# A hand-written order of 24 token blocks on five engines: a new order table, 11 transposed copies and 9 last sums moved to VectorE

## The chip, the cores and the metric

The kernel runs on one core of a Trainium2 chip. The metric is the device time of the core in microseconds (us), and the runs before have a median of 119.65 us (118.96 to 119.69, three runs). The profile used throughout is one execution of the same program, whose span is 118.6 us.

## What is computed

Windowed attention with four sink keys, followed by a highway layer. Cut to what matters:

```python
scores = q @ k.T / sqrt(64)          # 4 batches, 8 heads, 768 positions, head size 64
keep = (key < 4) | (0 <= row - key < 128)
a = softmax(where(keep, scores, -1e9))
x = (a @ v) as [3072 tokens, 512]
H = maximum(x @ w_h, 0)
T = 1 / (1 + exp(-(x @ w_t + b_t)))
out = T * H + (1 - T) * x            # float32
```

## The kernel before

The 3072 tokens are 24 blocks of 128, six to a batch. Each block goes through a fixed set of steps, and a table of text, `_STEPS`, lists every step of every block as `name:block`. The program is recorded in the order of that table, so each engine executes its own steps in exactly that order, and an instruction that waits holds up everything behind it on its engine. Buffers come from rotating pools.

The steps, with the lines of the profile and the engine:

- `lq`, `lk` load 128 rows of q and k for all heads (L151, GpSimd's queue, 128 KB each with a cast to f16; blocks 0 and 1 come through the SP and ACT queues, L144, and are cast on VectorE by `cvq`, `cvk`, L169). `lv` loads v of one block of batch 0 (L147), `lv0` and `lv1` half of v of a later batch (L157, 384 KB each). `lw_t`, `lw_h` load the weights (L181).
- `T` transposes q and k on TensorE (L267), `cT` copies the result to SBUF on ScalarE (L273).
- `S0`, `S1` are the scores of four heads each (TensorE, L317), `E0`, `E1` the exponentials (ScalarE, L325), `M0`, `M1` the multiplication by the mask (VectorE, L336, in place in `e`).
- `sk`, `es` and `pks` handle the sink keys; `pks` has two small copies (L284) and, from the second batch on, a product (L176) on GpSimd. `BA` opens the accumulations with the bias of the gate (L342) and the sink part (L350).
- `AV` is the product with v (TensorE, L370); `rec` and `x` divide by the sum (VectorE, L379, L384).
- `X` transposes x on TensorE (L395), `cX` copies the result from PSUM to SBUF on ScalarE (L406).
- `Tt` and `H` are the two products of the highway layer (TensorE, L416 and L428); `u` is a tanh on ScalarE (L421); `d`, `g`, `ee` are VectorE's part (L434, L441, L447).
- `o` is the last sum (L453), on GpSimd for all blocks but the last, which is on VectorE; the store to memory is issued on the SP queue behind it (L454).

`_FILL` adds idle matmuls on a constant tile in front of a few early steps. The pools that matter: 8 buffers each for the loaded q and k, 2 PSUM buffers that `T` and `S` share, one PSUM buffer that `AV` and `X` share, 2 PSUM buffers for `Tt`, `H`, the bias and `sk`, and 4 buffers for the last sum. GpSimd's loads use eight semaphores in turn, so a load is issued when the one eight places ahead of it has landed.

Of the kernel before, what the change touches and what calls it, by code (L numbers as in the profile page):

```python
# [11 lines left out]
ALU = mybir.AluOpType  # L12
# [6 lines left out]

_FILL = {'T:0': 4, 'S1:0': 3, 'T:1': 1, 'S1:1': 3, 'S0:1': 2, 'S1:2': 1, 'T:3': 3}  # L20
_STEPS = """
    lq:0 lk:0 lq:1 lk:1 K3:0 lsv:0 pm:0 K1:0 lbt:0 cvq:0 K4:0 cvk:0 lv:1 K2:0 lv:0 pb:0 T:0
    cvq:1 cT:0 S1:0 BA:1 cvk:1 S0:0 lq:2 E1:0 E0:0 M0:0 M1:0 T:1 lk:2 cT:1 lw_t:0 S1:1 T:2 lq:3
    lk:3 E1:1 M1:1 AV:0 pks:0 lw_h:0 lq:4 rec:0 x:0 cT:2 S0:1 E0:1 S1:2 M0:1 E1:2 X:0 lk:4 cX:0
    K5:0 lv:2 T:3 S0:2 AV:1 cT:3 Tt:0 E0:2 lv:3 S1:3 rec:1 u:0 x:1 X:1 E1:3 sk:2 M0:2 es:2 M1:2
    cX:1 H:0 T:4 d:0 S0:3 cT:4 M1:3 BA:2 lq:5 lk:5 AV:2 Tt:1 lv:4 lq:6 S1:4 E0:3 rec:2 x:2 X:2
    g:0 M0:3 lv:5 H:1 ee:0 u:1 lk:6 g:1 cX:2 lq:7 T:5 E1:4 BA:3 AV:3 d:1 S0:4 cT:5 rec:3 E0:4
    Tt:2 u:2 x:3 sk:4 es:4 S1:5 X:3 ee:1 M1:4 T:6 M0:4 cX:3 E1:5 g:2 lv0:6 H:2 lk:7 o:0 d:2
    BA:4 AV:4 S0:5 Tt:3 cT:6 rec:4 S1:6 x:4 ee:2 E0:5 lk:8 lq:8 X:4 u:3 H:3 T:7 M0:5 lq:9 M1:5
    cX:4 E1:6 BA:5 S0:6 cT:7 AV:5 d:3 Tt:4 E0:6 rec:5 x:5 S1:7 u:4 X:5 g:3 H:4 T:8 cX:5 E1:7  # L30
    ee:3 o:1 lv1:6 cT:8 BA:6 lk:9 M1:6 lq:10 o:2 M0:6 d:4 AV:6 lk:10 rec:6 S0:7 lq:11 x:6 M1:7
    Tt:5 E0:7 g:4 o:3 S1:8 M0:7 X:6 u:5 H:5 cX:6 BA:7 ee:4 T:9 AV:7 pks:6 d:5 E1:8 cT:9 rec:7
    S0:8 x:7 g:5 E0:8 Tt:6 lk:11 sk:8 S1:9 M1:8 X:7 T:10 u:6 M0:8 H:6 es:8 cX:7 o:4 BA:8 ee:5
    lq:13 d:6 E1:9 AV:8 rec:8 x:8 S0:9 cT:10 Tt:7 X:8 lq:12 lk:12 g:6 S1:10 H:7 E0:9 u:7 cX:8
    E1:10 T:11 M0:9 o:5 M1:9 BA:9 AV:9 lk:13 S0:10 ee:6 lv0:12 Tt:8 cT:11 d:7 sk:10 rec:9 E0:10
    x:9 o:6 u:8 X:9 S1:11 g:7 T:12 lk:14 M0:10 lq:15 ee:7 es:10 cX:9 H:8 E1:11 M1:10 BA:10 d:8
    lq:14 AV:10 rec:10 x:10 g:8 cT:12 S0:11 Tt:9 M1:11 E0:11 X:10 u:9 S1:12 o:7 M0:11 lv1:12
    cX:10 lk:15 H:9 BA:11 ee:8 T:13 E1:12 S0:12 cT:13 AV:11 d:9 rec:11 Tt:10 x:11 E0:12 lq:16
    u:10 S1:13 M0:12 X:11 H:10 g:9 T:14 cX:11 M1:12 o:8 BA:12 E1:13 ee:9 cT:14 lq:17 d:10 AV:12
    S0:13 Tt:11 rec:12 x:12 lk:16 o:9 M1:13 X:12 E0:13 M0:13 g:10 S1:14 u:11 T:15 H:11 cX:12  # L40
    AV:13 BA:13 ee:10 E1:14 d:11 pks:12 rec:13 S0:14 Tt:12 cT:15 x:13 lk:17 M1:14 sk:14 X:13
    S1:15 E0:14 g:11 u:12 es:14 T:16 H:12 cX:13 M0:14 ee:11 BA:14 E1:15 o:10 AV:14 d:12 rec:14
    S0:15 cT:16 x:14 g:12 lk:18 E0:15 Tt:13 X:14 u:13 M1:15 S1:16 lq:18 H:13 M0:15 T:17 lq:19
    cX:14 E1:16 g:13 cT:17 BA:15 ee:12 AV:15 S0:16 d:13 o:11 Tt:14 E0:16 rec:15 lv0:18 lk:19
    sk:16 x:15 u:14 ee:13 X:15 S1:17 cX:15 o:12 T:18 es:16 M0:16 lk:20 E1:17 M1:16 lq:20 lq:21
    g:14 H:14 BA:16 AV:16 S0:17 Tt:15 cT:18 d:14 S1:18 rec:16 x:16 E0:17 u:15 ee:14 M0:17 o:13
    X:16 H:15 T:19 cX:16 E1:18 lv1:18 BA:17 M1:17 cT:19 S0:18 AV:17 Tt:16 S1:19 d:15 rec:17
    E0:18 lk:21 o:14 x:17 g:15 X:17 u:16 M0:18 T:20 cX:17 M1:18 H:16 ee:15 E1:19 AV:18 BA:18
    d:16 rec:18 x:18 S0:19 Tt:17 cT:20 S1:20 E0:19 X:18 H:17 M1:19 u:17 T:21 M0:19 g:16 lq:22
    cX:18 ee:16 AV:19 BA:19 lk:22 E1:20 g:17 S0:20 o:15 cT:21 pks:18 rec:19 Tt:18 E0:20 d:17  # L50
    sk:20 x:19 u:18 M1:20 es:20 ee:17 S1:21 lq:23 X:19 cX:19 T:22 M0:20 E1:21 H:18 d:18 o:16
    BA:20 AV:20 rec:20 x:20 cT:22 S0:21 E0:21 Tt:19 X:20 M1:21 S1:22 g:18 u:19 H:19 cX:20 lk:23
    T:23 M0:21 BA:21 E1:22 g:19 ee:18 AV:21 o:17 S0:22 cT:23 E0:22 d:19 rec:21 Tt:20 sk:22 x:21
    u:20 es:22 X:21 S1:23 M1:22 cX:21 M0:22 ee:19 H:20 BA:22 E1:23 AV:22 g:20 d:20 S0:23 rec:22
    Tt:21 E0:23 x:22 M1:23 u:21 M0:23 X:22 H:21 cX:22 ee:20 BA:23 d:21 o:18 AV:23 rec:23 x:23
    g:21 ee:21 Tt:22 u:22 X:23 g:22 H:22 o:19 cX:23 Tt:23 d:22 H:23 ee:22 d:23 u:23 g:23 o:20
    o:21 ee:23 o:22 o:23
"""


# [1 line left out]
def kernel(  # L62
# [27 lines left out]
    NB = NT // P  # L90
# [164 lines left out]
    xtp_of, xh_of, xT_of, t_of, u_of, h_of, dd_of, ee_of, sk_of = {}, {}, {}, {}, {}, {}, {}, {}, {}  # L255
# [49 lines left out]
    def scores(n, g):  # L305
        qT, kT = qkT[n]
        srcs = ([] if n % NSC == 0 else [qkT[n - 1][1]]) + [kT]
        np_ = len(srcs)
        sps = s_ps.tile([P, 2, 512], FP32, tag="s", name="sps")
        fill(sps[:, 0, :], f"S{g}:{n}")  # L310
        for hl in range(2):
            hp = 2 * g + hl
            for pc, kk in enumerate(srcs):
                for hh in range(2):
                    rows = slice(64 * hh, 64 * hh + 64)
                    o = (hl * np_ + pc) * P
# [120 lines left out]

    def g(n):
        gt = td_pool.tile([P, DM], FP16, tag="gt", name="gt")
        eng = nc.gpsimd if False else nc.vector  # L440
        eng.tensor_scalar(out=gt, in0=u_of.pop(n), scalar1=0.5, scalar2=0.5,  # L441
                          op0=ALU.mult, op1=ALU.add)
        g_of[n] = gt

    def ee(n):
# [1 line left out]
        nc.vector.tensor_tensor(out=e, in0=g_of.pop(n), in1=dd_of.pop(n), op=ALU.mult)  # L447
# [63 lines left out]
```

## Time and profile before

| | |
|---|---|
| median of the runs | 119.65 us |
| span of the profiled execution | 118.6 us |
| TensorE matmul busy | 105.6 us (89%) |
| VectorE busy | 94.6 us (80%) |
| ScalarE busy | 93.3 us (79%) |
| GpSimd busy | 90.2 us (76%) |

The span is the time from the first to the last instruction of the program in the trace; the device time is about 1.0 us more (119.65 against 118.6). A row of a group says how long one instruction takes (mean), how often it occurs, and how long its engine was idle just ahead of it. From the groups, mean of one: `e` multiplied by the mask, 128x1024, 828 ns; the division `xh` 691 ns; `dd` 685 ns; `gt` 371 ns; `ee` 419 ns; the last sum on GpSimd 1188 ns, and on VectorE (block 23 alone) 691 ns; the copy `xT` on ScalarE 582 ns. The idle time ahead of an instruction counts only on the engine that sets the end.

### The profile page before, as it was taken

The page shows a single profiled execution, that of the slowest core. Times are in us where ns is not written, and L with a number is a line of the kernel's source. Part 1 is how long each engine was busy: PE and PEld are TensorE (multiplying, and loading weights), DVE is VectorE, ACT ScalarE, POOL GpSimd, SP SyncE. Part 2 cuts the span into 40 slices and gives each one's busy share as a digit, 9 for nine tenths or more (in the row PEclk, how much of TensorE's full clock was granted, in tenths as well). Part 3 has the DMA queues.
Part 4 walks back from the last instruction along what each step waited for, and adds up shares of the span by engine and source line. Part 5 has one row for each costly group of instructions (what it writes and reads, how often), then busy time and mean ns, then how long its engine had stood idle before and what let it go on. Part 6 is the DMA issues. An engine that isn't in the chain of part 4 may idle for free.

```text
span 118.6 us, 3872 instructions
## 1 busy us (share of the span) xinstructions
PE 105.6 (89%) x1617; PEld 57.7 (49%) x1617; DVE 94.6 (80%) x204; ACT 93.3 (79%) x129; POOL 90.2 (76%) x105
## 2 busy tenths in 40 slices
PE   5947899999996899999998999999699999999920
PEld 2313465556462456555554664555454664644300
DVE  5497458789899739688987997999989969878760
ACT  2137899899978479999989999999869999963410
POOL 5999995999999884969998799699949651233430
PEclk9999999999999679999999999999999999999999
DMA  2999999999999999899999999999999692220242
GB/s 49 248 171 182 173 194 154 161 150 151 196 211 172 224 122 135 131 100 194 159 165 205 162 136 116 177 197 161 151 212 152 44 144 85 94 88 0 88 177 88
DMA packets 79540, 17.56 MB, mean 148 GB/s; under 512 B 75426, under 2 KB 76450, under 8 KB 79524
## 3 DMA queue, kind: packets, MB, share of 16 engines
q0 software_dynamic: 71904, 9.98, 127.2%
q1 hardware_dynamic: 5540, 6.82, 16.6%
q10 hardware_dynamic: 2080, 0.52, 2.4%
q8 instruction: 12, 0.20, 0.7%
q14 instruction: 4, 0.03, 0.1%
HBM read 21.01 MB, written 6.29 MB: 230 GB/s over the span
## 4 chain that ended last, share of the span: by engine, by line
PE 37%; POOL 25%; DMA 20%; issue 7%; DVE 6%; ACT 1%; POOLq 0%; DVEq 0%
DMA vb<-in_v_dram 14%; PE hps L428 10%; PE tps L416 9%; POOL qsd L151 7%; DMA wh_sb<-in_moe_w_h_dram 6%; POOL ksd L151 6%; PE av L370 6%; PE sps L317 5%; POOL otok L453 5%; DVE e L336 3%; POOL vb L157 2%; POOL v_all L147 2%; PE xtp L395 2%; PE tp L267 2%; PE tps L342 2%
## 5 line engine op out<-in xcount | busy, mean ns | idle before, releaser
L325 ACT ACTIVATE e<-sps 128x1024 f16<-128x1024 f32 (+1 forms) x48 | 46.0, 964 | 4.6 <-PE sps L317 4.2
L453 POOL TENSOR_TENSOR otok<-xh,ee 128x512 f32<-128x512 f16 x23 | 27.3, 1188 | 20.1 <-DVE ee L447 16.9
L336 DVE TENSOR_TENSOR e<-e,mask 128x1024 f16<-128x1024 f16 (+1 forms) x48 | 36.4, 784 | 3.4 <-ACT e L325 3.1
L273 ACT COPY qk<-tp 128x1024 f16<-128x1024 f16 x24 | 24.5, 1022 | 6.3 <-PE tp L267 6.1
L416 PE MATMUL tps<-wt_sb,xT 128*128 128x512 f16 x96 | 25.5, 389 | 0.0
L428 PE MATMUL hps<-wh_sb,xT 128*128 128x512 f16 x96 | 25.4, 388 | 0.0
L434 DVE SCALAR_TENSOR_TENSOR dd<-hps,xh 128x512 f16<-128x512 f32 x24 | 16.4, 685 | 6.2 <-PE hps L428 6.1
L151 POOL DMA_DIRECT2D qsd<-in_q_dram x22 | 19.8, 902 | 1.0 <-DMA wh_sb<-in_moe_w_h_dram 1.0
L151 POOL DMA_DIRECT2D ksd<-in_k_dram x22 | 19.8, 898 | 0.0
L421 ACT ACTIVATE u<-tps 128x512 f16<-128x512 f32 x24 | 14.5, 603 | 6.4 <-PE tps L416 4.4
L317 PE MATMUL sps<-qk 64*128 64x128 f16 x352 | 18.8, 220 | 0.7 <-ACT qk L273 0.7
L384 DVE TENSOR_TENSOR xh<-av,rec 128x512 f16<-128x512 f32 x24 | 16.6, 691 | 0.8
L370 PEld LDWEIGHTS <-e 128*128 128x128 f16 x352 | 12.8, 97 | 8.2 <-issue 3.5
L317 PEld LDWEIGHTS <-qk 64*128 64x128 f16 x352 | 11.1, 95 | 7.9 <-issue 5.8
L370 PE MATMUL av<-vb,e 128*128 128x66 f16 x264 | 11.9, 194 | 2.9 <-DVE e L336 1.1
L406 ACT COPY xT<-xtp 128x512 f16<-128x512 f16 x24 | 14.0, 582 | 0.4 <-PE xtp L395 0.2
L416 PEld LDWEIGHTS <-xT 128*128 128x128 f16 x96 | 7.6, 98 | 7.9 <-issue 0.5
L428 PEld LDWEIGHTS <-xT 128*128 128x128 f16 x96 | 7.7, 99 | 7.7 <-issue 0.6
L447 DVE TENSOR_TENSOR ee<-gt,dd 128x512 f16<-128x512 f16 x24 | 10.1, 419 | 0.6
L379 DVE RECIPROCAL rec<-av 128x8 f32<-128x8 f32 x24 | 4.9, 205 | 6.5 <-PE av L370 6.5
L441 DVE TENSOR_SCALAR gt<-u 128x512 f16<-128x512 f16 x24 | 8.9, 371 | 0.0
L157 POOL DMA_DIRECT2D vb<-in_v_dram x6 | 8.8, 1462 | 0.2 <-issue 0.2
(65 smaller groups left out, 109.1 us busy)
## 6 DMA issues: line engine op xcount, KB each, us to landing
out_dram<-otok SPq DMA_DIRECT2D x24, 256.0 KB, 3.0
qsd<-in_q_dram POOLq DMA_DIRECT2D x22, 128.0 KB, 5.7
ksd<-in_k_dram POOLq DMA_DIRECT2D x22, 128.0 KB, 5.9
vb<-in_v_dram POOLq DMA_DIRECT2D x6, 384.0 KB, 7.1
v_all<-in_v_dram POOLq DMA_DIRECT2D x6, 128.0 KB, 7.4
kf<-in_k_dram ACTq DMA_DIRECT2D x2, 256.0 KB, 5.7
qf<-in_q_dram SPq DMA_DIRECT2D x2, 256.0 KB, 5.1
wt_sb<-in_moe_w_t_dram POOLq DMA_DIRECT2D x1, 512.0 KB, 6.4
```

The costliest lines, as they stand in the source:

```text
L151: nc.gpsimd.dma_start(out=sd, in_=dram(x, n))
L273: nc.scalar.copy(out=qk.rearrange("p j (a t) -> p a j t", a=2), in_=tp_of.pop(n)[:, :, 0:DM].rearrange("p a (j t) -> p a j t", t=64))
L317: nc.tensor.matmul(sps[:, hh, o:o + P], lhsT=kk[rows, hp, :], rhs=qT[rows, hp, :], start=True, stop=True)
L325: nc.scalar.activation(out=e.rearrange("p a b c d -> p a (b c d)"), in_=sps[:, :, 0:2 * np_ * P], func=AF.Exp, bias=_EXP_BIAS, scale=SCALE)
L336: nc.vector.tensor_tensor(out=ev, in0=ev, in1=m.unsqueeze(1).to_broadcast([P, 4, np_ * P]), op=ALU.mult)
L370: nc.tensor.matmul(av[:, g, 2 * hl + hh, 0:_AVN], lhsT=e[:, hh, hl, pc, :], rhs=v_cols(m, h), start=fresh, stop=False, skip_group_check=True)
L384: nc.vector.tensor_tensor(out=xh.rearrange("p (h d) -> p h d", d=D), in0=av_of.pop(n)[:, :, 0:D], in1=rec_of.pop(n).unsqueeze(2).to_broadc ...
L416: nc.tensor.matmul(t_of[n], lhsT=xT[:, kc, :], rhs=wt_sb[:, kc, :], start=False, stop=(kc == NOC - 1))
L421: nc.scalar.activation(out=uu, in_=t_of.pop(n), func=AF.Tanh, scale=0.5)
L428: nc.tensor.matmul(hps, lhsT=xT[:, kc, :], rhs=wh_sb[:, kc, :], start=(kc == 0), stop=(kc == NOC - 1))
L434: nc.vector.scalar_tensor_tensor(out=dd, in0=h_of.pop(n), scalar=0.0, in1=xh_of[n], op0=ALU.max, op1=ALU.subtract)
L453: eng.tensor_tensor(out=otok, in0=xh_of.pop(n), in1=ee_of.pop(n), op=ALU.add)
```

## The change

All steps stay, with the same tiles, buffers, idle matmuls and arithmetic. The table is a new one for all engines, two steps have a second form on VectorE, and two `if False` branches are gone.

- `cXd` is `cX` as a `tensor_copy` on VectorE, for blocks 1, 2, 7, 9, 11, 13, 15, 16, 17, 19 and 21. The other 13 stay on ScalarE.
- `od` is the last sum on VectorE, for blocks 0, 2, 3, 4, 5, 9, 12, 21, 22 and 23. Block 23 was there already, so 9 move and 14 stay on GpSimd. The store stays on the SP queue behind it.
- Most loads stand further ahead of the step that uses them, counted in steps of the table: for instance `lv1:6` 77 rather than 9, `lk:7` 89 rather than 18, `lq:10` 80 rather than 40. `lw_t` stands 47 steps ahead of `Tt:0` rather than 28, and behind seven other loads on GpSimd's queue rather than four.

```diff
 _STEPS = """
-    lq:0 lk:0 lq:1 lk:1 K3:0 lsv:0 pm:0 K1:0 lbt:0 cvq:0 K4:0 cvk:0 lv:1 K2:0 lv:0 pb:0 T:0
-    cvq:1 cT:0 S1:0 BA:1 cvk:1 S0:0 lq:2 E1:0 E0:0 M0:0 M1:0 T:1 lk:2 cT:1 lw_t:0 S1:1 T:2 lq:3
...
-    cX:4 E1:6 BA:5 S0:6 cT:7 AV:5 d:3 Tt:4 E0:6 rec:5 x:5 S1:7 u:4 X:5 g:3 H:4 T:8 cX:5 E1:7
-    ee:3 o:1 lv1:6 cT:8 BA:6 lk:9 M1:6 lq:10 o:2 M0:6 d:4 AV:6 lk:10 rec:6 S0:7 lq:11 x:6 M1:7
...
-    g:21 ee:21 Tt:22 u:22 X:23 g:22 H:22 o:19 cX:23 Tt:23 d:22 H:23 ee:22 d:23 u:23 g:23 o:20
-    o:21 ee:23 o:22 o:23
+    lsv:0 lq:0 lk:3 lq:2 lq:3 K4:0 lk:0 cvq:0 cvk:0 T:0 lq:1 cvq:1 lk:1 cT:0 lk:2 lv:0 S1:0 E1:0
+    pm:0 S0:0 K3:0 pks:0 cvk:1 lk:4 K1:0 lv:1 lbt:0 lw_t:0 lq:4 E0:0 M0:0 K2:0 M1:0 T:1 pb:0 lv:2
...
+    pks:6 g:3 cT:7 od:0 H:3 lq:11 lk:11 T:8 BA:5 od:2 AV:5 d:3 ee:3 cT:8 Tt:4 u:4 S1:6 E1:6 rec:5
+    od:3 x:5 S0:7 H:4 BA:6 M0:6 d:4 E0:7 X:5 S1:8 S1:7 M1:6 cX:5 Tt:5 g:4 ee:4 E1:8 od:4 lq:12 AV:6
...
+    u:22 x:23 X:23 cX:23 ee:21 H:22 od:21 g:22 d:22 Tt:23 ee:22 od:22 u:23 g:23 H:23 d:23 ee:23
+    od:23
 """
...
-    def cX(n):
+    def cX(n, eng=None):
         xT = x_pool.tile([P, NOC, P], FP16, tag="xT", name="xT")
         dst = xT.rearrange("p j (a t) -> p a j t", a=2)
         src = xtp_of.pop(n)[:, :, 0:NOC * 64].rearrange("p a (j t) -> p a j t", t=64)
-        if False:
-            nc.vector.tensor_copy(out=dst, in_=src)
+        if eng is not None:
+            eng.tensor_copy(out=dst, in_=src)
         else:
             nc.scalar.copy(out=dst, in_=src)
         xT_of[n] = xT
...
-    def o(n):
+    def o(n, eng):
         otok = o_pool.tile([P, DM], FP32, tag="otok", name="otok")
-        eng = nc.gpsimd if n < NB - 1 else nc.vector
         eng.tensor_tensor(out=otok, in0=xh_of.pop(n), in1=ee_of.pop(n), op=ALU.add)
         nc.sync.dma_start(out=out[n * P:(n + 1) * P, :], in_=otok)
...
-        "d": d, "g": g, "ee": ee, "o": o,
+        "cXd": lambda n: cX(n, nc.vector),
+        "d": d, "g": g, "ee": ee, "o": lambda n: o(n, nc.gpsimd), "od": lambda n: o(n, nc.vector),
```

More of the change, by code (lines that the diff above doesn't have):

```diff
@@ L21 @@
 _STEPS = """
-    lq:0 lk:0 lq:1 lk:1 K3:0 lsv:0 pm:0 K1:0 lbt:0 cvq:0 K4:0 cvk:0 lv:1 K2:0 lv:0 pb:0 T:0
-    cvq:1 cT:0 S1:0 BA:1 cvk:1 S0:0 lq:2 E1:0 E0:0 M0:0 M1:0 T:1 lk:2 cT:1 lw_t:0 S1:1 T:2 lq:3
[L24 to L27, printed above, removed]
@@ L28 @@
-    Tt:2 u:2 x:3 sk:4 es:4 S1:5 X:3 ee:1 M1:4 T:6 M0:4 cX:3 E1:5 g:2 lv0:6 H:2 lk:7 o:0 d:2
-    BA:4 AV:4 S0:5 Tt:3 cT:6 rec:4 S1:6 x:4 ee:2 E0:5 lk:8 lq:8 X:4 u:3 H:3 T:7 M0:5 lq:9 M1:5
-    cX:4 E1:6 BA:5 S0:6 cT:7 AV:5 d:3 Tt:4 E0:6 rec:5 x:5 S1:7 u:4 X:5 g:3 H:4 T:8 cX:5 E1:7
-    ee:3 o:1 lv1:6 cT:8 BA:6 lk:9 M1:6 lq:10 o:2 M0:6 d:4 AV:6 lk:10 rec:6 S0:7 lq:11 x:6 M1:7
-    Tt:5 E0:7 g:4 o:3 S1:8 M0:7 X:6 u:5 H:5 cX:6 BA:7 ee:4 T:9 AV:7 pks:6 d:5 E1:8 cT:9 rec:7
-    S0:8 x:7 g:5 E0:8 Tt:6 lk:11 sk:8 S1:9 M1:8 X:7 T:10 u:6 M0:8 H:6 es:8 cX:7 o:4 BA:8 ee:5
@@ L34 @@
[L34 to L55, printed above, removed]
-    g:21 ee:21 Tt:22 u:22 X:23 g:22 H:22 o:19 cX:23 Tt:23 d:22 H:23 ee:22 d:23 u:23 g:23 o:20
-    o:21 ee:23 o:22 o:23
+    lsv:0 lq:0 lk:3 lq:2 lq:3 K4:0 lk:0 cvq:0 cvk:0 T:0 lq:1 cvq:1 lk:1 cT:0 lk:2 lv:0 S1:0 E1:0
@@ new lines @@
+    pm:0 S0:0 K3:0 pks:0 cvk:1 lk:4 K1:0 lv:1 lbt:0 lw_t:0 lq:4 E0:0 M0:0 K2:0 M1:0 T:1 pb:0 lv:2
+    cT:1 S1:1 E1:1 M1:1 T:3 lw_h:0 S0:1 BA:1 lk:5 AV:0 rec:0 cT:3 T:2 E0:1 lq:5 x:0 X:0 cT:2 cX:0
+    lv:3 S0:2 E0:2 M0:1 S0:3 E0:3 lk:7 AV:1 K5:0 sk:2 es:2 lv:4 rec:1 x:1 S1:2 E1:2 X:1 M0:2 cXd:1
+    Tt:0 T:4 lk:6 cT:4 S1:3 lq:6 BA:2 E1:3 M0:3 M1:2 AV:2 rec:2 x:2 u:0 Tt:1 u:1 lv:5 S1:4 E1:4 lq:7
+    X:2 cXd:2 lq:8 lk:8 S0:4 M1:3 g:1 H:0 d:0 E0:4 g:0 H:1 T:5 cT:5 ee:0 BA:3 M1:4 Tt:2 u:2 lv0:6
+    lv1:6 d:1 ee:1 AV:3 S1:5 E1:5 S0:5 sk:4 es:4 rec:3 x:3 X:3 cX:3 g:2 H:2 lk:9 o:1 lq:9 M1:5 T:6
@@ new lines @@
+    lq:10 M0:4 BA:4 AV:4 E0:5 cT:6 d:2 rec:4 x:4 Tt:3 lk:10 ee:2 S0:6 u:3 M0:5 E0:6 T:7 X:4 cX:4
+    pks:6 g:3 cT:7 od:0 H:3 lq:11 lk:11 T:8 BA:5 od:2 AV:5 d:3 ee:3 cT:8 Tt:4 u:4 S1:6 E1:6 rec:5
+    od:3 x:5 S0:7 H:4 BA:6 M0:6 d:4 E0:7 X:5 S1:8 S1:7 M1:6 cX:5 Tt:5 g:4 ee:4 E1:8 od:4 lq:12 AV:6
+    rec:6 u:5 H:5 BA:7 x:6 M0:7 X:6 E1:7 cX:6 T:9 cT:9 lk:12 M1:7 S0:8 d:5 AV:7 rec:7 E0:8 g:5 Tt:6
+    u:6 sk:8 T:10 cT:10 x:7 M1:8 M0:8 lk:13 X:7 cXd:7 S0:9 lv1:12 es:8 H:6 E0:9 lq:14 S1:9 E1:9
+    lq:13 g:6 d:6 ee:6 o:6 BA:8 AV:8 Tt:7 S1:10 rec:8 x:8 X:8 M0:9 H:7 M1:9 u:7 g:7 cX:8 d:7 BA:9
@@ new lines @@
+    ee:5 E1:10 lq:15 T:11 AV:9 rec:9 x:9 S0:10 ee:7 Tt:8 cT:11 S0:11 od:5 X:9 E0:10 cXd:9 lk:14
+    M1:10 u:8 lv0:12 T:12 o:7 cT:12 pks:12 sk:10 H:8 es:10 S1:11 M0:10 d:8 E0:11 g:8 BA:10 AV:10
+    rec:10 x:10 lk:15 lk:20 lk:16 Tt:9 E1:11 ee:8 o:8 u:9 M1:11 M0:11 S0:12 E0:12 S1:12 g:9 X:10
+    cX:10 M0:12 H:9 d:9 T:13 cT:13 BA:11 AV:11 rec:11 x:11 E1:12 lq:19 Tt:10 ee:9 u:10 T:14 cT:14
+    BA:12 X:11 lq:16 S1:13 E1:13 lk:17 od:9 lq:17 lk:19 H:10 cXd:11 M1:12 lq:18 S0:13 d:10 E0:13
+    AV:12 rec:12 g:10 Tt:11 u:11 x:12 M0:13 S1:14 M1:13 g:11 ee:10 BA:13 X:12 cX:12 o:10 lk:18 T:15
@@ new lines @@
+    cT:15 E1:14 H:11 d:11 AV:13 rec:13 x:13 lv1:18 S0:14 E0:14 lq:20 Tt:12 ee:11 sk:14 u:12 S0:15
+    E0:15 M1:14 S1:15 M0:14 es:14 X:13 o:11 cXd:13 g:12 M0:15 H:12 d:12 T:16 E1:15 BA:14 AV:14
+    rec:14 x:14 lv0:18 T:17 ee:12 M1:15 cT:16 od:12 Tt:13 cT:17 X:14 u:13 g:13 H:13 d:13 ee:13 o:13
+    cX:14 S0:16 E0:16 S1:16 E1:16 BA:15 AV:15 Tt:14 S0:17 rec:15 x:15 u:14 M0:16 X:15 cXd:15 S1:17
+    M1:16 g:14 E0:17 M0:17 sk:16 es:16 H:14 E1:17 d:14 lk:21 T:18 BA:16 cT:18 AV:16 Tt:15 T:19
+    rec:16 x:16 X:16 S0:18 M1:17 H:15 cXd:16 u:15 lq:22 lq:21 g:15 E0:18 ee:14 cT:19 M0:18 lk:22
@@ new lines @@
+    d:15 S1:18 E1:18 o:14 BA:17 AV:17 rec:17 x:17 Tt:16 u:16 BA:18 ee:15 T:20 M1:18 X:17 cXd:17 o:15
+    g:16 S1:19 cT:20 H:16 d:16 S0:19 E1:19 AV:18 rec:18 x:18 ee:16 E0:19 M0:19 Tt:17 M1:19 u:17 T:21
+    g:17 pks:18 X:18 cX:18 cT:21 S1:20 E1:20 H:17 d:17 AV:19 rec:19 x:19 BA:19 lq:23 ee:17 M1:20
+    S0:20 E0:20 Tt:18 u:18 M0:20 sk:20 T:22 cT:22 es:20 X:19 g:18 H:18 cXd:19 S1:21 S0:21 E1:21
+    E0:21 d:18 ee:18 BA:20 AV:20 Tt:19 u:19 S1:22 rec:20 x:20 X:20 cX:20 M1:21 lk:23 M0:21 E1:22
+    g:19 H:19 d:19 T:23 cT:23 ee:19 BA:21 AV:21 rec:21 x:21 o:16 M1:22 Tt:20 u:20 g:20 S0:22 E0:22
@@ L58 @@
+    X:21 o:17 cXd:21 M0:22 sk:22 es:22 H:20 d:20 ee:20 S1:23 S0:23 BA:22 AV:22 E1:23 rec:22 x:22
+    E0:23 M0:23 Tt:21 u:21 o:18 X:22 cX:22 M1:23 g:21 H:21 o:19 d:21 BA:23 AV:23 rec:23 o:20 Tt:22
+    u:22 x:23 X:23 cX:23 ee:21 H:22 od:21 g:22 d:22 Tt:23 ee:22 od:22 u:23 g:23 H:23 d:23 ee:23
+    od:23
 """
@@ L439, in g @@
         gt = td_pool.tile([P, DM], FP16, tag="gt", name="gt")
-        eng = nc.gpsimd if False else nc.vector
-        eng.tensor_scalar(out=gt, in0=u_of.pop(n), scalar1=0.5, scalar2=0.5,
-                          op0=ALU.mult, op1=ALU.add)
+        nc.vector.tensor_scalar(out=gt, in0=u_of.pop(n), scalar1=0.5, scalar2=0.5,
+                                op0=ALU.mult, op1=ALU.add)
         g_of[n] = gt
```

## Prediction

> **What bounds the kernel now.** I read the busy shares first, then who waited for whom, then the busy time by stretches, and last VectorE's order of time where TensorE had waited.
>
> ```profile
> PE 105.6 (89%) x1617; PEld 57.7 (49%) x1617; DVE 94.6 (80%) x204; ACT 93.3 (79%) x129; POOL 90.2 (76%) x105
> PE tp L267 <- DVE kh L169: 1.3, 1, 1.3
> PE av L370 <- DVE e L336: 1.1, 1, 1.1
> PE av L370 <- ACT qk L273: 1.0, 1, 1.0
> PE av L370 <- DMA vb<-in_v_dram: 0.9, 2, 0.5
> 20.00:110.00 90.00, 86.51 (x1407) 48.84 (x1408) 77.92 (x151) 79.77 (x113) 70.49 (x74) 0.98 1.56 146
> 39.60:43.00 3.40, 3.40 (x23) 1.40 (x22) 2.37 (x5) 2.61 (x4) 2.22 (x3) 0.50 1.73 177
> ```
>
> The first line is the page's, four are the waits, two are stretches (length, busy PE, PEld, DVE, ACT, POOL, granted clock, DMA share, GB/s). From 20 to 110 us TensorE is busy for 86.5 of 90 us: it sets the pace, and only what makes it wait or slows it can change the time. In the chain of waits ten Tt groups lie between 65.11 and 105.80 us, 4.07 us for a block. VectorE is idle for 90 - 77.9 = 12.1 us of the same stretch, so it follows closely. The third wait has the wrong name: ACT's qk was long done, and the late one was VectorE's e, which ended at 38.01 us, ahead of the matmul at 38.07. After that hole TensorE had half its clock for 3.4 us.
>
> VectorE's order of time, in two places (start, length, then the groups; a row with x2 is two instructions):
>
> ```profile
> 69.55 0.68 DVE L336 TENSOR_TENSOR e<-e,mask 128x1024 f16<-128x1024 f16 x1
> 70.15 0.29 DVE L441 TENSOR_SCALAR gt<-u 128x512 f16<-128x512 f16 x1
> 70.35 0.69 DVE L336 TENSOR_TENSOR e<-e,mask 128x1024 f16<-128x1024 f16 x1
> 70.95 0.42 DVE L447 TENSOR_TENSOR ee<-gt,dd 128x512 f16<-128x512 f16 x1
> ...
> 82.44 3.21 DVE L336 TENSOR_TENSOR e<-e,mask 128x1024 f16<-128x1024 f16 x2
> 85.57 0.68 DVE L434 SCALAR_TENSOR_TENSOR dd<-hps,xh 128x512 f16<-128x512 f32 x1
> ```
>
> From start to start an undisturbed e costs 0.60 us, gt 0.20; two e's take 1.28. At 82.44 they take 3.21, with GpSimd busy beside them: a ksd issue at 83.02 and an otok sum at 83.92. I call this a hold. Such pairs: 2.25 at 26.78, 2.26 at 31.51, 1.54 at 65.67, 2.24 at 78.17, 3.21 at 82.44, 2.06 at 90.14, and 1.89 at 36.12 for two half-size ones (else 0.75). Over the undisturbed length that is 0.97 + 0.98 + 0.26 + 0.96 + 1.93 + 0.78 + 1.14 = 7.0 us. gt has a mean of 371 against a median of 286 ns, 24 times: 2.0 us more. Holds cost VectorE 9.0 us, and TensorE 2.1 of them (the waits of 1.1 and 1.0): 23%. The rest went into VectorE's idle time.
>
> **The change, part by part**, against the profiled span of 118.6 us (the median is 1.03 more).
>
> *Loads further ahead.* They can save the two waits for vb, 0.9 us: lv0:6 and lv1:6 now stand 78 and 77 steps ahead, not 54 and 9. T waited 0.3 us for a ksd, in the weight loads only, and TensorE not at all by that. Landings come one behind the other, about 0.87 us each for a 128 KB load, and a load waits for the one eight ahead, as GpSimd's wait of 1.0 us for wh shows. More steps are thus not more bandwidth, but vb's place moves ahead of others; I take -0.9 (0 to -0.9). On GpSimd's queue the loads pass otok sums, whose 16.9 us of waiting for ee leaves room; the stores on SP only follow them.
>
> *The half clock.* It followed 1.5 us of TensorE idle between 36.2 and 39.6 us (busy 1.90 of 3.40). Without that hole it does not come: 3.40 x 0.5 = -1.7 (0 if it returns elsewhere).
>
> *Start.* K3 and K1 leave the front of VectorE's order, so cvk no longer delays T:0: -1.3. But lw_t stands behind seven loads instead of four and lw_h behind three more, at 0.87 us each, so Tt:0 and H:0 come no earlier (wt landed at 13.4 us and Tt:0 began at 17.25; three loads more is 16.0, a margin of about 1). The early gain is idle time again until block 5: 0 (-1.3 to +1.0).
>
> *Tail.* g:23 leaves the place between d:23 and ee:23. There dd began at 113.40 and ee at 114.40, where dd alone needs 0.7: -0.3. od:21 and od:22 lie beside H:23: 0.
>
> *ACT.* 11 copies of 0.47 us (start to start) leave it: 5.2 us. TensorE waited for it only in the first 16 us, so 0 (to -0.5).
>
> *VectorE.* It gains 11 copies and 9 sums. A sum costs 0.69 us, 0.60 from start to start (otok on VectorE, block 23; xh and dd are the same). A copy from PSUM to f16 has no row; the nearest are xh, which reads 512 f32 of PSUM in 0.69, and e of 512 f16 elements in SBUF, 0.42. From start to start that is 0.34 to 0.60, and below nothing is excluded, since it is work added; I take the middle, 0.47, as the copy shares PSUM with the first row and type with the second. In the stretch from 20 to 110 us lie all 11 copies and seven sums: 3.7 to 6.6, plus 4.2, is 7.9 to 10.8 us. Of 12.1 us of idle 1.3 to 4.2 are left, say 2.75.
>
> [...]
>
> That idle time is what hid the holds. At 12.1 us of it TensorE pays 23%; with none it would pay all; in a straight line 2.75 us give 82%. Buffers hide some, so I take 70% (bounds 23% and 100%). Holds shrink a little: 3.1 of the 7.0 us lay beside GpSimd's sums and products (1.14, 0.26, 0.78 and half of 1.93), 2.1 of them otok's, and 9 of 23 otok go: -0.8, 8.2 remain. Then 0.7 x 8.2 - 2.1 = +3.6 (8.2 x 0.23 - 2.1 = -0.2 to +6.1).
>
> *Four sums in a row.* od:0, od:2, od:3 and od:4 stand within two blocks on VectorE, ahead of rec:5, x:5 and rec:6. A block costs VectorE 2 x 0.60 + 0.23 + 0.61 + 0.60 + 0.20 + 0.34 = 3.18, two with the sums 8.8, and TensorE 2 x 4.07 = 8.1: +0.7 (0 to +2.4). Behind od:3 wait x:5 and X:5. An od also waits for the store four sums back; stores landed 3.0 us after issue, so no wait.
>
> Sum: -0.9 - 1.7 + 0 - 0.3 + 0 + 3.6 + 0.7 = +1.4. 118.6 + 1.4 = 120.0, as device time 121.1.
>
> **Rivals.** First, *half the cover stays*: TensorE pays 45% of the holds, and half the price of the four sums: 8.2 x 0.45 - 2.1 = +1.6, +0.3; the sum is -1.0, and with the vb waits back -0.1: 118.7 to 119.6, no change. For it: no VectorE e has to be early in most blocks, as 77% was hidden so far. Against: 2.75 us of idle over 22 blocks.
>
> Second, *the holds leave with GpSimd's sums* (faster). If what holds VectorE is GpSimd reading SBUF, then only 3.1 + 2.0 us are such holds, and fewer sums mean fewer of them. The holds then stay hidden as now: -0.2, no price for the four sums, and the sum is -0.9 - 1.7 - 0.3 - 0.2 = -3.1: 115.5, device time 116.5; with some price for the four sums 117.2. It decides where VectorE keeps over about 5 us idle. Against it: the pairs at 26.78 and 31.51 lay beside load issues alone, and were held 0.97 and 0.98 us.
>
> [...]
>
> Third, *the half clock comes back*, since X:5 and AV:6 wait in the same stretch for the four sums: forecast plus 1.7, 122.8. A sum on VectorE reads two SBUF tiles as e does, and can be held like it: 7 of 48 e's were, so one or two of nine, +1.3 more.
>
> **How the numbers follow.** About 1% is what a measurement here tells from no change: 118.45 to 120.85. Forecast with the third rival: 0.46, of which 0.12 has the half clock back; half the cover: 0.27; holds leaving: 0.27. The forecast is the likeliest, 121.1. The range goes from 117.2 (a tenth left out below) to 124.0 (forecast + 1.7 + 1.3, a tenth above). Faster 0.27, same 0.27, slower 0.46.
>
> **What would show it.** VectorE busy well over 100 us, with less than 4 us idle between 20 and 110; TensorE waiting for xh, e and dd of VectorE, 4 to 6 us in all; no wait for vb; no stretch at half clock; xT on VectorE between 0.42 and 0.69 us. I am wrong if the pairs of e stay near 1.28, or if TensorE's waits for VectorE stay near 2 us: then the second rival holds. A wait of Tt:0 or H:0 for a weight would make the start's term wrong.

## The result, and the profile after

| | before | changed |
|---|---|---|
| median of the runs | 119.55 us (118.96 to 119.69) | 123.16 us (122.52 to 123.58) |
| ratio | | 1.031, 95% interval 1.026 to 1.036 |
| span of the profiled execution | 118.6 us | 121.9 us |
| TensorE busy, 20 to 110 us | 86.5 us | 82.3 us |
| VectorE busy, 20 to 110 us | 77.9 us | 83.7 us |
| GpSimd busy, all | 90.2 us | 80.9 us |

The change makes the kernel 3.1% slower; 1.2% was forecast. Ratios here and below compare the faster executions of each kernel, while the traces of the new order alone and of it with one move, of the sums alone in the old order, and of the short sums in the changed kernel and in the kernel before are of executions over 1.5% above that kernel's fastest. From the page of the kernel before, the chain that ended last, by engine; then from that of the changed kernel, the busy shares and the same chain:

```profile
PE 37%; POOL 25%; DMA 20%; issue 7%; DVE 6%; ACT 1%; POOLq 0%; DVEq 0%
...
PE 103.4 (85%) x1617; PEld 56.5 (46%) x1617; DVE 106.0 (87%) x224; ACT 88.8 (73%) x118; POOL 80.9 (66%) x96
DVE 48%; DMA 22%; PE 19%; POOL 5%; issue 3%; SPq 0%; DVEq 0%; POOLq 0%
```

VectorE passes TensorE in busy share, and the chain that ends last is VectorE's for 48% of the span; in the kernel before it was VectorE's for 6% and TensorE's for 37%. The waits of TensorE (total, times, longest):

```profile
PE av L369 <- DVE e L335: 3.2, 4, 1.6
PE xtp L394 <- DVE xh L383: 3.1, 7, 0.9
PE tps L415 <- DMA wt_sb<-in_moe_w_t_dram: 1.4, 1, 1.4
PE tp L266 <- DMA qsd<-in_q_dram: 1.3, 1, 1.3
```

Of before, the waits for vb are gone. A wait of T for q (block 9, at 43.58 us) and one of Tt:0 for its weight have come, and x's product and the masked e are late eleven times. Gap by gap from 20 us on (gaps over 0.15 us), TensorE stood waiting for VectorE 5.8 us, against 2.2 before, the misnamed one with them. The largest gap, in the order of time of VectorE, GpSimd and TensorE:

```profile
91.63 3.10 DVE L335 TENSOR_TENSOR e<-e,mask 128x1024 f16<-128x1024 f16 x2
...
91.17 0.94 POOL L150 DMA_DIRECT2D qsd<-in_q_dram  x1
92.10 0.89 POOL L150 DMA_DIRECT2D ksd<-in_k_dram  x1
93.00 1.17 POOL L450 TENSOR_TENSOR otok<-xh,ee 128x512 f32<-128x512 f16 x1
...
94.79 0.42 PE L369 MATMUL av<-vb,e 128*128 128x66 f16 x8 [1.61 <-DVE e L335]
```

Two e's take 3.10 us in place of 1.28, with two load issues and a last sum beside them, and TensorE stands for 1.61. Summed over e, gt and ee, against their undisturbed 0.60, 0.20 and 0.34 us, the holds come to 12.0 us, where they were 8.9. The same kernel before has 10.8 us of them in its second trace (below), so that only a part of this growth is clear of the change from execution to execution. By stretches (length, busy PE, PEld, DVE, ACT, POOL, clock, DMA share, GB/s):

```profile
20.00:110.00 90.00, 82.31 (x1371) 46.49 (x1367) 83.71 (x161) 74.15 (x99) 63.27 (x68) 0.98 1.68 150
...
95.00:98.50 3.50, 3.50 (x53) 2.50 (x50) 3.47 (x6) 1.85 (x3) 1.54 (x1) 0.71 0.43 94
98.50:101.00 2.50, 2.50 (x28) 1.01 (x28) 1.62 (x5) 1.53 (x3) 0.00 (x0) 0.72 0.27 105
```

Behind that gap a lower clock comes (0.71 and 0.72 in the last two stretches), as the third rival had it, but in another place. It is not in every execution: the three other runs have mean clocks of 0.989 to 0.993 (this one 0.980) and spans of 120.8 to 121.5 us.

### The profile page after: what moved, and what is told of

Its sections match the earlier page's. It is cut to its first block, busy times and chain, and to the rows that moved or that the text cites. A ratio compares the mean times of both kernels' runs of the same rounds, so it can differ in the third digit from the quotient of the medians.

```text
span 121.9 us, 3856 instructions
## 1 busy us (share of the span) xinstructions
PE 103.4 (85%) x1617; PEld 56.5 (46%) x1617; DVE 106.0 (87%) x224; ACT 88.8 (73%) x118; POOL 80.9 (66%) x96
## 4 chain that ended last, share of the span: by engine, by line
DVE 48%; DMA 22%; PE 19%; POOL 5%; issue 3%; SPq 0%; DVEq 0%; POOLq 0%
DVE e L335 17%; DMA qsd<-in_q_dram 9%; DVE dd L433 8%; DMA wh_sb<-in_moe_w_h_dram 8%; DVE xh L383 7%; PE hps L427 6%; DMA qf<-in_q_dram 5%; DVE ee L445 5%; DVE gt L439 4%; PE tps L415 3%; PE av L369 3%; PE sps L316 2%; DVE otok L450 2%; DVE rec L378 2%; PE tp L266 2%
## 5 line engine op out<-in xcount | busy, mean ns | idle before, releaser
L324 ACT ACTIVATE e<-sps 128x1024 f16<-128x1024 f32 (+1 forms) x48 | 44.5, 953 | 5.6 <-PE sps L316 5.5
L335 DVE TENSOR_TENSOR e<-e,mask 128x1024 f16<-128x1024 f16 (+1 forms) x48 | 38.1, 815 | 0.1
L450 POOL TENSOR_TENSOR otok<-xh,ee 128x512 f32<-128x512 f16 x14 | 17.3, 1238 | 20.8 <-DVE ee L445 19.8
L415 PE MATMUL tps<-wt_sb,xT 128*128 128x512 f16 x96 | 24.8, 380 | 1.7 <-DMA wt_sb<-in_moe_w_t_dram 1.4
L316 PE MATMUL sps<-qk 64*128 64x128 f16 x352 | 16.6, 218 | 0.8 <-ACT qk L272 0.7
L369 PEld LDWEIGHTS <-e 128*128 128x128 f16 x352 | 12.7, 97 | 8.4 <-DVE e L335 4.4
L316 PEld LDWEIGHTS <-qk 64*128 64x128 f16 x352 | 10.5, 94 | 10.7 <-issue 9.6
L445 DVE TENSOR_TENSOR ee<-gt,dd 128x512 f16<-128x512 f16 x24 | 10.7, 446 | 0.8
L394 PE MATMUL xtp<-ident,xh 64*128 64x64 f16 x192 | 7.3, 194 | 3.4 <-DVE xh L383 3.1
L439 DVE TENSOR_SCALAR gt<-u 128x512 f16<-128x512 f16 x24 | 9.5, 396 | 0.0
L341 PE MATMUL tps<-bt,ones_row 64*128 64x512 f16 x23 | 8.7, 379 | 0.2 <-DVE dd L433 0.2
(66 smaller groups left out, 121.5 us busy)
```

Source lines behind the costliest of these rows:

```text
L335: nc.vector.tensor_tensor(out=ev, in0=ev, in1=m.unsqueeze(1).to_broadcast([P, 4, np_ * P]), op=ALU.mult)
L369: nc.tensor.matmul(av[:, g, 2 * hl + hh, 0:_AVN], lhsT=e[:, hh, hl, pc, :], rhs=v_cols(m, h), start=fresh, stop=False, skip_group_check=True)
L415: nc.tensor.matmul(t_of[n], lhsT=xT[:, kc, :], rhs=wt_sb[:, kc, :], start=False, stop=(kc == NOC - 1))
```

## The experiments

Theory A was the prediction's: VectorE's added work takes the cover of its holds. Theory B: the new order costs the time, and the moved work is what it was balanced for. Every ratio is to the kernel before, run on the same chip.

| kernel | ratio | 95% interval |
|---|---|---|
| changed | 1.031 | 1.026 to 1.036 |
| new order alone | 1.051 | 1.047 to 1.055 |
| new order, sums moved, copies not | 1.050 | 1.045 to 1.055 |
| new order, copies moved, sums not | 1.047 | 1.040 to 1.054 |
| old order, copies and sums moved | 1.019 | 1.017 to 1.022 |
| old order, copies moved | 1.014 | 1.009 to 1.019 |
| old order, sums moved | 1.011 | 1.006 to 1.017 |

**New order alone.** `cXd` becomes `cX`, and `od` becomes `o` but for block 23.

```diff
-    lv:3 S0:2 E0:2 M0:1 S0:3 E0:3 lk:7 AV:1 K5:0 sk:2 es:2 lv:4 rec:1 x:1 S1:2 E1:2 X:1 M0:2 cXd:1
+    lv:3 S0:2 E0:2 M0:1 S0:3 E0:3 lk:7 AV:1 K5:0 sk:2 es:2 lv:4 rec:1 x:1 S1:2 E1:2 X:1 M0:2 cX:1
...
-    pks:6 g:3 cT:7 od:0 H:3 lq:11 lk:11 T:8 BA:5 od:2 AV:5 d:3 ee:3 cT:8 Tt:4 u:4 S1:6 E1:6 rec:5
+    pks:6 g:3 cT:7 o:0 H:3 lq:11 lk:11 T:8 BA:5 o:2 AV:5 d:3 ee:3 cT:8 Tt:4 u:4 S1:6 E1:6 rec:5
```

> The new table, but all 24 copies of x's transpose on ScalarE and all last sums but block 23's on GpSimd. Theory A (VectorE's added work took the cover of the holds): TensorE's waits for VectorE after 20 us fall from the 5.8 us of the changed kernel to about the 2.0 us of before, so the ratio to before falls from 1.031 to 1.00 (119.0 to 120.2 us). Theory B (the order itself costs the time, the moved work is only what it was balanced for): the ratio stays at 1.03 or goes above it, and TensorE's waits move to ScalarE (the scores waiting for a copy of q and k that now stands behind a copy of x's transpose) or to GpSimd's holds.

1.051: theory A falls as the account of the new order, since VectorE has no added work here and the kernel is slower still. TensorE's waits in this trace:

```profile
PE xtp L394 <- DVE xh L383: 3.7, 7, 1.2
PE av L369 <- DVE e L335: 2.9, 4, 1.1
...
PE av L369 <- ACT qk L272: 1.1, 1, 1.1
PE av L369 <- ACT xT L405: 0.7, 1, 0.7
PE sps L316 <- ACT e L324: 0.6, 1, 0.6
```

The waits for VectorE stay. The third row is one more of them, named wrongly as its like was in the kernel before: an e ended just ahead of that matmul. The last two are ScalarE's and are new. The holds are 18.2 us, against the 8.9 and 10.8 of the two traces of before.

**The moves in the old order.** The table of before with the same blocks' `cXd` and `od`, then with each kind alone.

> The table of before, with only the 11 copies and the 9 sums on VectorE, each at the place it has now. Theory A: the copies cost 11 x 0.34 and the sums 9 x 0.60 = 9.1 us of VectorE, of its 12.1 us of idle time, so the holds reach TensorE: ratio 1.02 to 1.03 (122 to 123.2 us). Theory B: the old order carries the work, ratio 0.995 to 1.01, and the waits of TensorE for VectorE stay under 3 us.

> The table of before with only the 11 copies on VectorE, 11 x 0.34 = 3.7 us more of its time. Together the copies and sums cost 0.019 in the old order. By their share of the added time (3.7 of 9.1 us) the copies cost 0.008; if VectorE's added time is harmless by itself and the order of the sums is what costs, 1.00.

> The table of before with only the nine sums on VectorE, 9 x 0.60 = 5.4 us more of its time, and GpSimd without nine sums of 1.19 us. By share of the added time 1.011; if fewer sums on GpSimd mean fewer held e's and gt's, which weighs against it, 0.99 to 1.005.

1.019, 1.014 and 1.011. In the old order the moved work does cost, the copies more than their share of time. The first is at the low edge of theory A's range, with 2.9 us of TensorE's waits for VectorE, which theory B had. Much of what the sums cost is the tail: `od:21`, `od:22` and `od:23` are VectorE's last work there, and from the end of H:23 the span runs 6.23 us in both traces with the sums moved, against 5.26 before. That is 1.0 of the 1.4 us that the sums alone cost. In the trace with the copies alone TensorE has half its clock from 7.6 to 14.4 us (mean 0.959 over the span); how much of the 1.4% that is was not taken apart. With the sums alone the holds fell to 6.1 us, as the second half of that expectation had it, but TensorE then waited 2.1 us for vb.

**Each move in the new order.**

> The changed kernel with the 11 copies of x's transpose back on ScalarE, the sums stay on VectorE. Theory A: 11 x 0.34 = 3.7 of VectorE's 9.1 us leave it, a bit under half the waits with them: ratio 1.015 (1.01 to 1.02). Theory B: ScalarE, 74.2 of 90 us busy in the middle, gets 11 x 0.47 = 5.2 us back and the scores wait for it: 1.03 or more.

> The changed kernel with its nine sums back on GpSimd; the 11 copies stay on VectorE. In the new order the copies alone were worth 0.020 (1.050 with the sums on VectorE, 1.031 with both) and the sums nothing (1.051 against 1.050). If these worths simply add, this kernel is at 1.03, as the changed one. If moved sums only pay where VectorE also has the copies (beside a sum on GpSimd 24 of 42 e's and 12 of 16 gt's were held, beside a load 19 of 167 and 31 of 61), it is at 1.04 or more.

1.050 and 1.047, against 1.051 with neither and 1.031 with both: neither move alone wins much, both together 0.020. The worths do not add. Why was not taken apart further; with the sums back on GpSimd the holds are 20.7 us.

**Weights first.** The two weight loads stand earlier on GpSimd's queue.

```diff
-    lsv:0 lq:0 lk:3 lq:2 lq:3 K4:0 lk:0 cvq:0 cvk:0 T:0 lq:1 cvq:1 lk:1 cT:0 lk:2 lv:0 S1:0 E1:0
-    pm:0 S0:0 K3:0 pks:0 cvk:1 lk:4 K1:0 lv:1 lbt:0 lw_t:0 lq:4 E0:0 M0:0 K2:0 M1:0 T:1 pb:0 lv:2
-    cT:1 S1:1 E1:1 M1:1 T:3 lw_h:0 S0:1 BA:1 lk:5 AV:0 rec:0 cT:3 T:2 E0:1 lq:5 x:0 X:0 cT:2 cX:0
+    lsv:0 lq:0 lk:3 lq:2 lq:3 K4:0 lk:0 cvq:0 cvk:0 T:0 lq:1 cvq:1 lk:1 cT:0 lk:2 lv:0 lw_t:0 S1:0 E1:0
+    pm:0 S0:0 K3:0 pks:0 cvk:1 lk:4 K1:0 lv:1 lw_h:0 lbt:0 lq:4 E0:0 M0:0 K2:0 M1:0 T:1 pb:0 lv:2
+    cT:1 S1:1 E1:1 M1:1 T:3 S0:1 BA:1 lk:5 AV:0 rec:0 cT:3 T:2 E0:1 lq:5 x:0 X:0 cT:2 cX:0
```

> The changed kernel with the two weight loads earlier on GpSimd's queue: w_t ahead of the two sink copies (which wait for ScalarE's first copy until 8.15 us), w_h right behind v's second block. Theory of the start: Tt:0 and H:0 no longer wait for 18.87 and 23.44 us; they come at about 17.3 and 20, and the 1.2 us by which block 3 is late against before go: ratio 1.02 (1.015 to 1.025). Rival: the time saved is lost again at the first later wait (the q load for block 9, 1.3 us), ratio 1.03 as now.

1.024 (1.021 to 1.027): the size came, the place did not. H:0 ends at 24.40 us against 24.52, since T:4 now waits 1.2 us for its q. What went is the wait of 1.3 us for the q of block 9. In the changed kernel GpSimd's order of time begins so:

```profile
8.15 0.72 POOL L283 COPY ks<-qk 64x16 f16<-64x16 f16 x2 [0.73 <-DVE ks L229]
...
11.14 0.79 POOL L180 DMA_DIRECT2D wt_sb<-in_moe_w_t_dram  x1
```

and its chain, where it runs over loads (start, length from issue to landing):

```profile
14.24 9.20 DMA wh_sb<-in_moe_w_h_dram
...
32.25 11.28 DMA qsd<-in_q_dram
```

The sink copies wait, by this row for VectorE's clearing of `ks` (K3) and not for ScalarE as I had written. w_t is issued at 11.14 us, 4.1 us later than before (7.01): three more loads ahead of it are 2.7 us of issues, and the copies with their wait and the load of v's sink rows behind them another 2.0, while two small steps of 0.5 us went behind it. Behind it w_h lands at 23.44 us, where it was 18.61, and a q load issued at 32.25 us takes 11.28 us from issue to landing.

**Loads alone.** The order of before, with the loads from block 6 on where the new table has them.

```diff
-    cX:1 H:0 T:4 d:0 S0:3 cT:4 M1:3 BA:2 lq:5 lk:5 AV:2 Tt:1 lv:4 lq:6 S1:4 E0:3 rec:2 x:2 X:2
+    cX:1 H:0 lk:6 lq:6 T:4 d:0 S0:3 cT:4 M1:3 BA:2 lq:5 lk:5 AV:2 Tt:1 lq:7 lq:8 lk:8 lv:4 S1:4
```

> The order of before on all engines, but the loads of q and k from block 6 on and of v from batch 1 on stand where they stand in the new table (by the TensorE work ahead of them); weights, the first blocks' loads and all other steps as before. If the earlier loads are what the new order pays for (GpSimd's issues and the landings one behind the other, with a new wait of T for a q load): 1.02 to 1.05. If it is the order of the other steps: 0.99 to 1.01, with the two waits for vb (0.9 us) gone at best.

1.019 (1.013 to 1.024). The waits for vb went; T now waits 1.3 us for q and 0.8 for k of block 5, which stand behind three loads of blocks 6 and 7 that are not needed yet. The holds rose to 12.8 us.

**Short sums.** GpSimd's sums are cut, in the changed kernel, then with a fill behind each, in the new order alone, and in the kernel before. They are also written to four tiles of their own, apart from those of VectorE's sums; in the changed kernel's list of waits no sum on VectorE waits for a tile. The stores keep their size.

```diff
-        eng.tensor_tensor(out=otok, in0=xh_of.pop(n), in1=ee_of.pop(n), op=ALU.add)
+        eng.tensor_tensor(out=otok[:, 0:w], in0=xh_of.pop(n)[:, 0:w], in1=ee_of.pop(n)[:, 0:w], op=ALU.add)
+        if w < DM:
+            eng.memset(idle, 0.0)
```

(w is 512 for the first four sums on GpSimd and 8 for the rest; the last two lines are those of the fill.)

> The changed kernel, in which GpSimd's last sums of ten blocks (10, 11 and 13 to 20) cover 8 of the 512 columns and the rest of those output rows is left out; everything else, the stores and VectorE's work and order too, as in the changed kernel. If the holds of VectorE beside GpSimd's sums are what reaches TensorE (the pairs at 59.5, 73.5, 91.6 and 97.2 us, with 0.96, 0.96, 1.81 and 0.96 us of hold, and gt at 61.1 with 0.96), the waits of TensorE after 57 us (4.7 us in all in the changed kernel) fall to 2 or less: ratio 1.00 to 1.015. If VectorE's added work alone makes it late, they stay, and the ratio stays at 1.025 to 1.031.

> As the kernel with the short sums, but behind each short sum GpSimd fills a spare 128x512 f32 tile with zeros: it is busy again, but writes only. If only GpSimd's reads hold VectorE: no e or gt held beside these fills, and the same ratio as with the short sums. If any GpSimd work does: e's and gt's held beside the fills, and a ratio nearer to the changed kernel's 1.031.

> The new order alone (all copies on ScalarE, all sums but block 23's on GpSimd, measured at 1.051), in which GpSimd's sums of 19 blocks cover 8 of the 512 columns and the rest of those rows is left out. If the new order costs what it costs because GpSimd's sums stand beside more of VectorE's fast instructions (18.2 us of holds against 8.9 of before): 1.00 to 1.015. If the order has other costs of its own (the scores behind ScalarE's copies, the loads): 1.03 to 1.045.

> The kernel before with the same 19 sums cut to 8 columns, the rest of those rows left out. In its trace two waits of TensorE of 1.0 and 1.06 us stand behind pairs of e that were held beside a sum. If the old order hides most of its holds: 0.98 to 0.99, so a gain of 2 us or less, and the difference between the two orders with short sums is the cost of the order without holds. If its holds cost it as much as they cost the new order: 0.96.

| | with full sums | with short sums |
|---|---|---|
| changed | 1.031 | 0.997 (0.992 to 1.001) |
| changed, fill behind each short sum | | 0.987 (0.980 to 0.994) |
| new order alone | 1.051 | 1.005 (1.001 to 1.010) |
| before | 1.000 | 0.984 (0.978 to 0.990) |

VectorE's instructions and their order are untouched, and 3.4% goes from the changed kernel, 4.6% from the new order alone, 1.6% from the kernel before. The last two are as expected, the first went a little below its range (1.00 to 1.015), and the kernel with fills, expected at the same ratio, lies lower still; the wait for the q of block 9 is gone from its trace. TensorE's waits in the new order alone with short sums:

```profile
PE xtp L394 <- DVE xh L383: 2.1, 4, 1.1
...
PE av L369 <- ACT xT L405: 1.0, 2, 0.8
PE av L369 <- DVE e L335: 0.8, 1, 0.8
```

By these lists the waits for x's product and e fall from 7.7 us (the misnamed one with them) to 2.9, those for ScalarE stay; the holds fall from 18.2 to 6.1. In the changed kernel with short sums the two largest waits for VectorE (0.9 and 1.6 us) are gone. A shorter sum also frees GpSimd's queue, so this alone would not settle it. The fill speaks against that rival: from 20 to 110 us GpSimd is busy for 60.7 us again (63.3 in the changed kernel, 55.5 with short sums alone), and no time is lost by it. Its order of time in two places, VectorE's row and GpSimd's:

```profile
72.51 0.70 DVE L335 TENSOR_TENSOR e<-e,mask 128x1024 f16<-128x1024 f16 x1
...
72.62 1.10 POOL L461 MEMSET idle<- 128x512 f32 x1
...
92.91 1.29 DVE L335 TENSOR_TENSOR e<-e,mask 128x1024 f16<-128x1024 f16 x2
...
93.59 0.52 POOL L461 MEMSET idle<- 128x512 f32 x1
```

Both e rows are undisturbed (0.70 for one, 1.29 for two) with a fill beside them; the first fill took 1.10 us, where an undisturbed one takes 0.52. These are the only two e's that met a fill. Of two gt's that did, one took 0.11 us longer. That GpSimd's writes alone hold nothing thus rests on these two e's and one of two gt's. The fill is shorter than a sum (0.59 against 1.19 us), so equal occupancy was not tried.

**Four sums in a row.** `od:0`, `od:2`, `od:3`, `od:4` become `o`.

> The changed kernel with only the sums of blocks 0, 2, 3 and 4 back on GpSimd. The prediction priced these four in a row on VectorE at 0.7 us. If so: 1.025. If they cost nothing: 1.031 as now; if they are cover like the other moved sums (in the new order, sums back on GpSimd made it 0.016 slower with nine): 1.035 to 1.04.

1.029 (1.020 to 1.038): too wide to part from 1.031, so no price of these four is shown. Its trace has waits for VectorE at 42.3 and 44.1 us of about 1.1 each, where the changed kernel has 0.4 and the wait for q.

**The kernel before, again.**

> The kernel before, unchanged, for a second trace. The span of its profiled execution on file was 118.6 us with a stretch at half clock; its other runs span 117.0 to 117.8 us. If the half clock is not part of a typical execution: span near 117.5 us, no stretch of 3 us at half clock between 20 and 110 us, so that there was nothing to win by its leaving. If it is typical: a stretch at half clock again behind the hole at 38 us, and 118.6 us.

The span is 117.1 us. The stretches of the prediction in this trace:

```profile
20.00:110.00 90.00, 86.14 (x1416) 48.72 (x1414) 80.15 (x154) 80.37 (x113) 70.94 (x75) 1.00 1.56 149
36.20:39.60 3.40, 1.90 (x36) 1.12 (x36) 2.79 (x5) 1.91 (x3) 3.26 (x6) 1.00 2.13 198
39.60:43.00 3.40, 3.40 (x65) 2.00 (x62) 2.93 (x7) 3.40 (x5) 2.22 (x3) 1.00 1.70 174
```

The same hole, 1.90 us busy of 3.40, and a full clock behind it. The first trace had caught a longer execution: its 118.6 us of span and the 1.7 us that each listed run has outside its span make 120.3, above each of the three runs behind the median of 119.65, though 21 of the 85 executions of this kernel listed beside the experiments span as much or more.

**Two sums, and v earlier, in the old order.** Three attempts at a better version, from the two holes of before: `o:3` and `o:14` become `od`; the same with `lv1:6` ahead of `lq:9` and `lv1:12` ahead of `lq:15`; and those two loads alone.

> The kernel before with only the sums of blocks 3 and 14 on VectorE: those two stood beside the pairs of e ahead of its two waits of 1.0 and 1.06 us (sums at 36.4 and 82.5 us). Holds go by place: both waits shrink by about 1 us each, two sums of 0.60 are added: 0.985 to 0.995, faster than both kernels. Rival: the loads that follow on GpSimd move up into the place of the sums and hold the same pairs: 1.00 to 1.01.

> The kernel before with the sums of blocks 3 and 14 on VectorE (measured at 0.996 alone: the waits for e shrank, but the wait for v's second half grew to 1.55 us), and the second half of v one load further ahead for batch 1 (ahead of q of block 9) and two further ahead for batch 2 (ahead of q of blocks 15 and 14). One load is 0.87 us, so the wait of 1.55 falls to 0.7 or less, and the one of 0.5 us goes: 0.98 to 0.99, faster than both kernels. Rival: the shifted issues hold other pairs of e: 1.00.

> The kernel before with only these two v loads moved. What loads further ahead are worth by themselves: the waits for vb are 0.5 and 0.4 us in the second trace of before: 0.99 to 0.995 if nothing else becomes late. If e, which ends at the same time as the wait for vb, is late anyway: 1.00.

0.996 (0.992 to 1.001), 0.998 (0.996 to 1.001), 0.997 (0.994 to 1.000). With the two sums moved, TensorE's wait for e left the list and this one grew from 0.9:

```profile
PE av L370 <- DMA vb<-in_v_dram: 2.5, 3, 1.5
```

With v earlier as well, vb left the list, and this came at another place (VectorE, then GpSimd):

```profile
32.32 3.22 DVE L335 TENSOR_TENSOR e<-e,mask 128x1024 f16<-128x1024 f16 x2
...
32.01 0.92 POOL L150 DMA_DIRECT2D ksd<-in_k_dram  x1
32.92 0.89 POOL L150 DMA_DIRECT2D qsd<-in_q_dram  x1
33.80 1.18 POOL L450 TENSOR_TENSOR otok<-xh,ee 128x512 f32<-128x512 f16 x1
```

A pair of e's is held 1.94 us and TensorE waits 1.5 us at 35.6. With the two loads alone vb left the list as well, and e came in its place:

```profile
PE av L369 <- DVE e L335: 3.0, 3, 1.5
```

For the second and third attempt the rival held: moving GpSimd's work moves the holds. In the first the wait for e went and v came late. No version that computes the whole output is clearly faster than the kernel before.

## Why the prediction was half right

The direction, the measured time within the range, and the sign of TensorE's waits for VectorE held. Step by step:

- **VectorE holds share and four sums in a row, +4.3 together.** TensorE's waits for VectorE grew by 5.8 - 2.2 = 3.6 us. The size was about right, and in part by luck: I had TensorE pay 70% of 8.2 us of holds, and it paid 48% of 12.0 (5.8 us). I let the cost come from VectorE's lost idle time and let the holds shrink by 0.8. They did not shrink: 12.0 us, where the two traces of before have 8.9 and 10.8, and the order without the moves has 18.2, of which TensorE pays 38% with no work added to VectorE. Nor does the sum of the holds set the price: the old order with v earlier has 12.7 us of them, lets 3.2 through and stands at 0.997. What the short sums show is that in the new order more than half of the time lost goes with GpSimd's sums beside VectorE's e and gt; why this order lets more of its holds through than the old one was not taken apart. VectorE kept 90 - 83.7 = 6.3 us idle, not 2.75. A copy takes 0.41 us and costs 0.34 from start to start, not 0.47: the cheap end of my range.
- **The half clock, -1.7: the step that failed most.** It was taken from one execution as if every run had it. The second trace has the hole without it, so nothing was there to win against the median. With this term at 0 the forecast is 122.8 us, close to the 123.16 measured. The same error is in the offset: device time is span plus 1.7, not plus 1.03.
- **Loads further ahead, -0.9.** The vb waits went and a wait of 1.3 for q came, +0.4 in sum. In the old order the new places of the loads cost 1.9% by themselves. I had written that more steps are not more bandwidth, and still took the whole gain.
- **Start, 0.** Here I counted the loads ahead of the weights, 2.7 of the 4.1 us by which w_t was issued later, and missed the sink copies on GpSimd's queue. It landed at 18.8 us, not at 16.0, and Tt:0 waited 1.4 us for it. What the place of the weights cost, some 0.7% by the medians, was paid at block 9.
- **Tail, -0.3.** From the end of H:23 the span ran 5.26 us before and 5.05 after: -0.2. Added up, 3.6 + 0 + 0.4 - 0.2 = +3.8 us, where the medians differ by 3.6.
- **ACT, 0.** Right in the old order, wrong in the new: there TensorE waits for ScalarE if the copies stay on it (0.7 and 0.6 us in the new order alone), so the moved copies have a use that I gave them no credit for.
- **What had no term:** the order of the steps itself. With GpSimd's sums short, new order and old still stand at 1.005 and 0.984, 2.1% apart. Of the order's 5.1%, 3.0 (4.6 - 1.6) thus go with GpSimd's sums. For the changed kernel the same difference is 1.8 (3.4 - 1.6) of its 3.1%, though ten sums were cut there and 19 in the kernel before. The rest is loads, weights and ScalarE, by the waits of the traces; it was not split further.

Among the rivals, "the holds leave with GpSimd's sums" was right that the sums hold VectorE (in the new order alone the holds fall from 18.2 to 6.1 us with short sums), with the wrong sign: nine sums left, but the others met more of VectorE's work. The third, with its lower clock and 122.8 us, came nearest by its number; the lower clock came at another place, and not in every execution. Its 1.3 us for held sums on VectorE did not come: the ten took 0.67 to 0.69 us each. No rival covers the e's held beside load issues alone, 19 of 167 in the traces of the last section.

## What to carry to other kernels

Before a stretch of a profile becomes a term, look whether a second execution has it; here one stretch that the second lacks made -1.7 us out of nothing. When an order moves, count for each engine what now runs beside what, since an engine with idle time to spare can still be held (VectorE and GpSimd had 6.3 and 26.7 us idle of 90 here, and the holds of VectorE came to 12.0), and price a load by all that stands ahead of it on its queue, which made w_t 4.1 us later here. To test a suspected hold, shorten the other engine's work and leave the victim's order alone.

## What the hardware showed that was not expected

Counted over six traces (before, changed, new order alone, both moves in the old order, weights first, sums alone in the new order): e was held in 24 of 42 cases beside a sum alone, in 19 of 167 beside load issues alone, in none of 56 with GpSimd idle; gt in 12 of 16, 31 of 61 and none of 58. (Held is over 0.1 us longer than undisturbed, and beside is what GpSimd did in the time that the instruction needs undisturbed. All 43 held e's are of the full size; of the half size none of 8 and none of 31 was held.) The instructions that read PSUM (xh and dd, 288 in all; 0.64 to 0.69 us in the traces of before and of the changed kernel) were never held. Of 55 holds of a full-size e 22 have one size, 0.95 to 0.98 us, and three are nearly twice that (1.9 in the trace of before). And the clock behind the same hole was 0.50 in one execution of the kernel before and 1.00 in another. In the clock records of two traces the stretch at half clock ahead of the last matmul is 3.41 us long and begins 34.13 us behind the first record (before, ten times 3.41) and 92.16 us behind it (changed, 27 times); the first record stands 5.5 and 4.3 us into the span. But in the two traces of before the stretch with the hole has TensorE busy alike (1.90 of 3.40 us in both), so what made the difference stays open. No run here varied it.
